# Key transposes of a pooled-attention kernel: one DMA transpose per head pair in place of one for two pairs

## The chip, the cores and the metric

The kernel runs on one core of one Trainium2 chip. The metric is the device time of one execution in microseconds (us). Five runs of the kernel before gave 418.2 to 424.3 us, with a median of 421.87 us. One execution was recorded by the hardware profiler, and every duration below comes from that execution or from its trace.

In the text PE is the matmul engine (TensorE), DVE the vector engine, ACT the scalar engine, POOL the GpSimd engine, and SP the sync engine, which here only issues DMAs. PEld is the weight load of PE.

## The reference, cut to what matters

Attention with queries pooled by two, over 8 batches, 8 heads, 1152 positions and head size 64, and then a feed-forward network with a product of two projections:

```python
q_pool = q.reshape(B, H, S // 2, 2, D).mean(axis=3)          # 576 pooled queries
scores = (1 / sqrt(D)) * q_pool @ k.transpose(0, 1, 3, 2)    # 576 x 1152 per head
attn = exp(scores - max) / sum
x = (attn @ v).transpose(0, 2, 1, 3).reshape(4608, 512)
out = ((x @ w1) * (x @ w2)) @ w3 @ w_out                     # 4608 x 512
```

Inputs and output are 32-bit floats. The kernel computes in 16-bit floats and sums in 32 bits.

## The kernel before, in words

**Tiling.** Two heads of one batch make a pair, so there are 32 pairs. For a pair, `scores` multiplies keys by pooled queries on PE (line 292). Both operands must have the head dimension on the partitions: `kT` holds the transposed keys of a pair (9 blocks of 128 columns; head 0 in partitions 0 to 63, head 1 in 64 to 127) and `qT` the transposed pooled queries. `expo` takes the exponential on ACT (line 302) of a chunk of 2 x 512 scores, `attend` multiplies the result by the values on PE (line 317), and `normalize` divides by the sum on DVE (lines 330, 334) and writes the result transposed into `xT` with DMA transposes from SP (lines 342, 345). The feed-forward network takes `xT` in units of 512 rows: `pa` and `pb` (line 411), their product `gT` (line 423), and the output rows `pp` (line 429), stored by SP (line 450).

**The order of the work.** It is written out by hand. The main loop has 108 iterations; each has three chunks of scores and exponentials, a listed number of `attend` matmuls, and up to two feed-forward groups. No engine reorders anything: each works through its own instructions in the order in which the loop emitted them, and waits at the first whose inputs are not ready. The framework derives the waits from the regions of tiles that an instruction reads and writes.

**How keys and queries get there.** Pairs 0 to 7 are transposed on PE. From pair 8 on two pairs P and P+1 are prepared together, by `prep_dma` (line 137), emitted about 1.95 pairs of scores ahead of pair P. In order, it does this:

1. `pool_q` (line 122), on POOL, adds neighbouring queries of both pairs into one tile `qp`.
2. Two copies on POOL (line 142), one for each pair, put the loaded keys `kst` into the block order of `kc`. Each waits for the landing of its own pair's keys.
3. SP issues one DMA transpose of `kc` into `kT` for both pairs (line 145, 18 blocks of 128 x 128) and then one of `qp` into `qT` (line 148, 9 blocks, since the two pairs' queries share partitions).

After it, `settled` (line 152) has POOL copy one element of `kT[P]` into a scratch cell. The value is not used; the copy makes POOL wait until the keys have landed transposed. Only then does POOL issue `load_two` for the next two pairs: two query loads, two value loads and two key loads (lines 82, 96, 89), which cast from 32 to 16 bits on the way. So POOL, SP and the DMA engines run a cycle, one turn for two pairs: loads, key copies, key transpose, the one-element copy, the next loads. `kc` has one buffer, `kT` and `qT` have two, `kst` and `vst` four.

Of the kernel before, what the change touches and what calls it, by code (L numbers as in the profile page):

```python
# [23 lines left out]
def kernel(  # L24
# [11 lines left out]
    nc = tc.nc  # L36
# [38 lines left out]
    kst, vst, qst, kT, qT, kTs, qTs, qps = {}, {}, {}, {}, {}, {}, {}, {}  # L75
# [38 lines left out]
    def pool_q(P, n=1):  # L114

        eng = nc.gpsimd if n == 2 else nc.vector
        pp, o = P // 2, 64 * (P % 2)
        if P % 2 == 0 or P == 1:
            qps[pp] = ab.tile([128, NJ, 2, D], FP16, tag="qp", bufs=2, name="qp")
        r = slice(o, o + 64 * n)  # L120
        src = qst[pp][r].rearrange("p u (c two) d -> p u c two d", two=2)
        eng.tensor_tensor(  # L122
            out=qps[pp][r].rearrange("p c u d -> p u c d"),
            in0=src[:, :, :, 0, :], in1=src[:, :, :, 1, :], op=ALU.add)

    def new_kq(P):
        if P % 2 == 0:
            kTs[P // 2] = ab.tile([128, 2, NJ, 128], FP16, tag="kT", bufs=2, name="kT")
            qTs[P // 2] = ab.tile([128, NJ, 128], FP16, tag="qT", bufs=2, name="qT")
        o = 64 * (P % 2)  # L130
        kT[P] = kTs[P // 2][:, P % 2]
        qT[P] = qTs[P // 2][:, :, o:o + 64]
# [4 lines left out]
    def prep_dma(P):  # L137

        pool_q(P, 2)
        for p in (P, P + 1):  # L140
            new_kq(p)
            nc.gpsimd.tensor_copy(  # L142
                out=new_kc(p).rearrange("p j u d -> p u j d").bitcast(mybir.dt.int32),
                in_=kst.pop(p).bitcast(mybir.dt.int32))
        nc.sync.dma_start_transpose(
            out=kTs[P // 2].rearrange("p t j f -> p (t j) f"),
            in_=kc2[P // 2].rearrange("p t j u d -> p (t j u d)"))
        nc.sync.dma_start_transpose(
            out=qTs[P // 2], in_=qps[P // 2].rearrange("p c u d -> p (c u d)"))

    def settled(P):
        nc.gpsimd.tensor_copy(out=seen, in_=kT[P][0:1, 0, 0:1])
# [1 line left out]
    kcs, kc2 = {}, {}  # L154

    def new_kc(P):
        if P % 2 == 0:
            kc2[P // 2] = ab.tile([128, 2, NJ, 2, D], FP16, tag="kc", bufs=1, name="kc")
        kcs[P] = kc2[P // 2][:, P % 2]
        return kcs[P]  # L160
# [241 lines left out]
    def ffn_groups(t):  # L402
# [70 lines left out]
        out=ident, in_=ident, compare_op=ALU.not_equal, fill=1.0,  # L473
# [102 lines left out]
    for it in range(NIT):  # L576
# [23 lines left out]
        if prepped < NPE:  # L600
            if it >= first_it(prepped) - (1 if prepped < 5 else 2):
                queue[0:0] = prep_groups(prepped)
                prepped += 1
                urgent = True
        elif prepped < NP and at >= prepped - 1.95:
            prep_dma(prepped)
            if loaded < NP:
                settled(prepped)
                load_two(loaded)
                loaded += 2  # L610
            prepped += 2
# [65 lines left out]
```

## Time and profile before

| what | before |
|---|---|
| median of 5 runs | 421.87 us (418.2 to 424.3) |
| profiled execution, its own time | 422.98 us |
| span of the profiled execution | 421.2 us |
| granted TensorE clock | 0.999 |
| PE busy | 409.2 us, 97% of the span |
| ACT busy | 326.9 us, 78% |
| DVE busy | 196.4 us, 47% |
| POOL busy | 121.0 us, 29% |
| moved by DMA | 59.76 MB |

The span is the stretch between the first and the last instruction that the profiler recorded; the execution's own time is 1.8 us more. "Busy" leaves out the time in which an engine only waits, branches or issues a DMA. The page also names a chain of work that ended last. It is found by going back from the last instruction to what released it, step by step, and where an engine waited even a little for a DMA, the chain goes off into what that DMA had waited for. So a large share of a line in the chain tells that work hangs on that line; it does not tell how long anyone waited for it. That stands in the view of waits, which adds up for every pair of waiter and releaser how long the waiter was idle.

### The profile page before, as it was taken

To read this page: it belongs to the slowest core of one execution; us is meant where nothing else is said; L and a number is where in the kernel's file an instruction comes from. 1 tells how busy PE (TensorE), PEld (TensorE's weight loads), DVE (VectorE), ACT (ScalarE), POOL (GpSimd) and SP (SyncE) were. 2 spreads that over 40 slices of the span, in tenths; PEclk is the share of its full clock that TensorE was granted. 3 is DMA by queue.
4 is the path that set the end of the run, shared out by engine and by line. 5 is a ranking of instruction groups with operands and counts; after the bars stand their busy time and mean duration, and the time that the engine had idled before them with its cause. 6 is when DMAs were issued, how large, how long until landed. Compare 5 with 4: busy or idle time off the path is not lost.

```text
span 421.2 us, 12709 instructions
## 1 busy us (share of the span) xinstructions
PE 409.2 (97%) x5507; PEld 272.3 (65%) x5507; DVE 196.4 (47%) x407; ACT 326.9 (78%) x357; POOL 121.0 (29%) x161
## 2 busy tenths in 40 slices
PE   8989999999999999999999999999999999999996
PEld 5567777766676577666765676666765866544443
DVE  2345656464545553555454534544455534613140
ACT  4899998988888888988888889897888889133332
POOL 6543431343434242331514242434333100000000
PEclk9999999999999999999999999999999999999999
DMA  8999999597989999897989998998989851050404
GB/s 188 202 207 193 200 205 202 99 150 129 171 147 190 142 154 173 128 161 134 130 129 206 136 178 159 175 137 152 182 145 155 133 125 23 14 115 2 100 2 100
DMA packets 95801, 59.76 MB, mean 142 GB/s; under 512 B 65152, under 2 KB 86144, under 8 KB 95744
## 3 DMA queue, kind: packets, MB, share of 16 engines
q0 software_dynamic: 26928, 32.97, 51.3%
q1 hardware_dynamic: 68656, 25.84, 35.1%
q8 instruction: 43, 0.70, 0.7%
q10 hardware_dynamic: 160, 0.13, 0.1%
q14 instruction: 14, 0.11, 0.1%
HBM read 67.11 MB, written 9.44 MB: 182 GB/s over the span
## 4 chain that ended last, share of the span: by engine, by line
DMA 60%; PE 24%; POOL 8%; ACT 3%; issue 2%; SPq 1%; DVE 1%; POOLq 0%; ACTq 0%
DMA kst<-in_k_dram 32%; DMA kT<-kc 15%; DMA qst<-in_q_dram 7%; PE pa L411 5%; PE pp L429 5%; PE pb L411 5%; DMA vst<-in_v_dram 4%; PE psc L292 3%; PE po L317 3%; ACT er L302 3%; POOL qst L82 2%; POOL kc L142 2%; POOL vst L96 2%; DMA er<-in_k_dram 1%; DMA qT<-qp 1%
## 5 line engine op out<-in xcount | busy, mean ns | idle before, releaser
L302 ACT ACTIVATE er<-psc 128x1024 f16<-128x1024 f32 x324 | 307.5, 1028 | 43.9 <-PE psc L292 43.6
L317 PEld LDWEIGHTS <-er 128*128 128x128 f16 x2880 | 103.3, 97 | 21.9 <-issue 5.8
L317 PE MATMUL po<-vt,er 128*128 128x65 f16 x2880 | 110.3, 193 | 0.0
L292 PE MATMUL psc<-qT,kT 64*128 64x512 f16 (+7 forms) x1152 | 96.7, 288 | 4.6 <-ACT er L302 2.2
L423 DVE TENSOR_TENSOR gT<-pb,asb 128x512 f16<-128x512 f32 x72 | 49.8, 692 | 56.4 <-PE pb L411 55.7
L411 PE MATMUL pa<-xT,w1sb 128*128 128x512 f16 x288 | 74.2, 380 | 0.0
L411 PE MATMUL pb<-xT,w2sb 128*128 128x512 f16 x288 | 74.1, 380 | 0.0
L429 PE MATMUL pp<-T,gT 128*128 128x256 f16 (+1 forms) x488 | 67.9, 292 | 0.0
L292 PEld LDWEIGHTS <-kT 64*128 64x128 f16 x1152 | 45.6, 94 | 29.2 <-issue 10.2
L429 PEld LDWEIGHTS <-gT 128*128 128x128 f16 x488 | 45.7, 98 | 18.5 <-issue 3.7
L421 DVE COPY asb<-pa 128x512 f32<-128x512 f32 x56 | 38.7, 692 | 39.9 <-PE pa L411 38.8
L411 PEld LDWEIGHTS <-w2sb 128*128 128x128 f16 x288 | 26.4, 98 | 32.7 <-issue 3.9
L411 PEld LDWEIGHTS <-w1sb 128*128 128x128 f16 x288 | 25.1, 98 | 30.1 <-issue 6.2
L122 POOL TENSOR_TENSOR qp<-qst 128x1152 f16<-128x1152 f16 x12 | 28.2, 2354 | 46.8 <-DMA qst<-in_q_dram 33.8
L441 DVE TENSOR_SCALAR osb<-pp 128x256 f32<-128x256 f32 x49 | 20.8, 425 | 39.3 <-PE pp L429 33.2
L330 DVE RECIPROCAL rz<-po 128x5 f32<-128x5 f32 x64 | 12.4, 194 | 50.2 <-PE po L317 49.8
L142 POOL COPY kc<-kst 128x576 int32<-128x576 int32 x24 | 16.1, 671 | 58.0 <-DMA kst<-in_k_dram 58.0
L334 DVE TENSOR_TENSOR xn<-po,rz 128x320 f16<-128x320 f32 x64 | 31.5, 492 | 2.5 <-DVE rz L330 0.3
L96 POOL DMA_DIRECT2D vst<-in_v_dram x32 | 23.4, 742 | 11.2 <-DMA w3h<-in_moe_w_dram 3.0
L438 ACT ACTIVATE osb<-pp 128x512 f32<-128x512 f32 (+1 forms) x12 | 7.0, 579 | 24.0 <-PE pp L429 20.6
L89 POOL DMA_DIRECT2D kst<-in_k_dram x31 | 22.8, 751 | 9.2 <-DMA kst<-in_k_dram 2.6
L419 ACT COPY asb<-pa 128x512 f32<-128x512 f32 x16 | 9.4, 585 | 16.5 <-PE pa L411 16.5
(42 smaller groups left out, 151.5 us busy)
## 6 DMA issues: line engine op xcount, KB each, us to landing
vst<-in_v_dram POOLq DMA_DIRECT2D x32, 288.0 KB, 10.2
out_dram<-osb SPq DMA_DIRECT2D x70, 128.0 KB, 2.5
kst<-in_k_dram POOLq DMA_DIRECT2D x31, 288.0 KB, 12.3
qst<-in_q_dram POOLq DMA_DIRECT2D x31, 288.0 KB, 6.6
w3h<-in_moe_w_dram POOLq DMA_DIRECT2D x3, 512.0 KB, 15.0
xT<-in_moe_w_out_dram POOLq DMA_DIRECT2D x4, 256.0 KB, 10.2
w1sb<-in_moe_w_dram POOLq DMA_DIRECT2D x2, 512.0 KB, 15.7
w2sb<-in_moe_w_dram POOLq DMA_DIRECT2D x2, 512.0 KB, 16.9
```

Source lines behind the costliest of these rows:

```text
L89: nc.gpsimd.dma_start(out=kst[P].rearrange("p u j d -> p u (j d)"), in_=k[b, h0:h0 + 2].rearrange("u (p j) d -> p u (j d)", j=NJ))
L96: nc.gpsimd.dma_start(out=vst[P].rearrange("p u j d -> p u (j d)"), in_=v[b, h0:h0 + 2].rearrange("u (p j) d -> p u (j d)", j=NJ))
L122: eng.tensor_tensor(out=qps[pp][r].rearrange("p c u d -> p u c d"), in0=src[:, :, :, 0, :], in1=src[:, :, :, 1, :], op=ALU.add)
L142: nc.gpsimd.tensor_copy(out=new_kc(p).rearrange("p j u d -> p u j d").bitcast(mybir.dt.int32), in_=kst.pop(p).bitcast(mybir.dt.int32))
L292: nc.tensor.matmul(t[:, u, o:o + ln].rearrange("p (c f) -> p c f", f=64), kT[P][s, j, :], qT[P][s, f0 // 64:(f0 + ln) // 64], start=True, ...
L302: nc.scalar.activation(out=er[:, :, r:r + CH], in_=psc.pop(c), func=AF.Exp, bias=0.0, scale=SCALE)
L317: nc.tensor.matmul(po[P, u][:, VW * x:VW * x + D + 1], er[:, u, r:r + 128], vts[P % 4][:, u, j, 0:D + 1], start=(m == 0), stop=(m == 44), ...
L334: nc.vector.tensor_tensor(out=xn[:, P % 2, :, u, :], in0=acc[:, :, 0:D], in1=rz.to_broadcast([128, 5, D]), op=ALU.mult)
L411: nc.tensor.matmul(p, w[:, mc, ft * 128:ft * 128 + 128], xT[:, mc, t0:t0 + 512], start=(mc == 0), stop=(mc == NC - 1))
L421: nc.vector.tensor_copy(out=asb[ft], in_=p)
L423: nc.vector.tensor_mul(out=gT[:, ft, :], in0=p, in1=asb.pop(ft))
L429: nc.tensor.matmul(p[:, 0:n], gT[:, ft, 128 * i:128 * i + 128], T16[:, ft, n * s:n * s + n], start=(ft == 0), stop=(ft == NF - 1))
```

## The change

In `prep_dma` the one DMA transpose of the keys of two pairs becomes two, one for each pair, and the transpose of the queries, which came after the keys, now stands between them. `settled(P)`, which is not edited, reads the first element of `kT[P]`, which the first of the two writes. Loads, copies, tiles, buffers and the place of `prep_dma` in the loop stay as they are.

```diff
@@ prep_dma @@
             nc.gpsimd.tensor_copy(
                 out=new_kc(p).rearrange("p j u d -> p u j d").bitcast(mybir.dt.int32),
                 in_=kst.pop(p).bitcast(mybir.dt.int32))
-        nc.sync.dma_start_transpose(
-            out=kTs[P // 2].rearrange("p t j f -> p (t j) f"),
-            in_=kc2[P // 2].rearrange("p t j u d -> p (t j u d)"))
-        nc.sync.dma_start_transpose(
-            out=qTs[P // 2], in_=qps[P // 2].rearrange("p c u d -> p (c u d)"))
+        for p in (P, P + 1):
+            nc.sync.dma_start_transpose(
+                out=kT[p], in_=kcs[p].rearrange("p j u d -> p (j u d)"))
+            if p == P:
+                nc.sync.dma_start_transpose(
+                    out=qTs[P // 2], in_=qps[P // 2].rearrange("p c u d -> p (c u d)"))
```

## The prediction

> **What bounds the kernel now.** I first read the busy times, then the waits, then the chain. The table of stretches, cut at 80 us (the first DMA transposes) and at 357 us (the last scores), gives for each engine its busy time:
>
> ```profile
> core 0: us, PE busy (x) PEld busy (x) DVE busy (x) ACT busy (x) POOL busy (x), PEclk, DMA share, GB/s
> 80.00:357.00 277.00, 275.06 (x3963) 186.79 (x3961) 135.87 (x278) 239.34 (x253) 89.58 (x113) 1.00 0.95 147
> ```
>
> In the 277 us in which the changed lines run, PE is idle for 277.00 − 275.06 = 1.94 us, at a clock of 1.00. The waits of PE alone, in the same stretch, have one line only:
>
> ```profile
> PE psc L292 <- DMA qT<-qp: 1.9, 4, 1.0
> ```
>
> Scores waited four times for the transposed queries. So PE, with 99.3% of the stretch, sets the pace. The change takes no work from PE, so at most these 1.94 us can be had. But the waits of all engines, and those of SP's queue, show that a second thing runs nearly as slowly:
>
> ```profile
> POOL seen L152 <- DMA kT<-kc: 62.7, 11, 6.6
> POOL kc L142 <- DMA kst<-in_k_dram: 58.0, 22, 5.8
> ...
> SPq L145 <- POOL kc L142: 121.8, 12, 12.8
> ```
>
> POOL waits 62.7 us for key transposes and 58.0 us for keys: no work of its own, but the cycle of loads and transposes going round. The chain, in order of time, shows one turn of it (start, duration, what):
>
> ```profile
> 283.78 0.68 POOL kc L142
> ...
> 284.47 4.67 DMA kT<-kc
> ...
> 289.26 0.18 POOL seen L152
> ...
> 289.72 1.25 POOL qst L82 x2
> 290.98 1.44 POOL vst L96 x2
> 292.42 0.68 POOL kst L89
> 293.09 11.85 DMA kst<-in_k_dram
> ```
>
> The keys of the second pair are copied, both pairs are transposed (4.67 us), POOL sees it and issues six loads, the last of which lands 15.2 us after the first was issued. From the issue of the key transpose for pair 16 (169.57 us) to that for pair 30 (330.14 us) seven turns take 160.57 us, 22.94 each. PE begins the scores of pair 16 at 180.24 and those of pair 30 at 337.74; less the 1.92 us of waits this is (157.50 − 1.92) / 7 = 22.23 per turn. So the cycle is 0.7 us a turn slower than PE. It used up its lead: the queries of pairs 8 to 16 landed 2.5 to 5.8 us before their scores, those of pairs 18, 22, 26 and 30 at the moment of use, with PE idle for 0.16, 0.31, 1.05 and 0.40 us. The page's 97% of PE and this cycle are both near the bound, and **the sign of the change hangs on whether the cycle gets shorter or longer**.
>
> **The change part by part.** Issue time on SP first:
>
> ```profile
> L145 SPq DMA_TRANSPOSE kT<-kc x12: 2652/2712/3817, 81.5 to 330.1; - x12
> ...
> DMA to landing us min/median/max: 4.7/5.2/6.5
> ...
> L148 SPq DMA_TRANSPOSE qT<-qp x12: 1350/1370/1629, 84.2 to 332.9; - x12
> ...
> DMA to landing us min/median/max: 3.3/4.5/4.8
> ```
>
> 18 blocks take 2.71 us to issue and 9 blocks 1.37, so two transposes of 9 cost 2 x 1.37 = 2.74: 0.03 us more, nothing. A transpose of 9 key blocks isn't in the trace; the query transpose has the same number and size of blocks and lands after 3.3 to 4.8, so I take that row. *Above*, the price is that of a transpose beside loads (below).
>
> *The first key transpose* needs only the first copy. For pair 26 that copy ended at 283.43 and the second at 284.45, so it is issued 1.0 us earlier. Over the last eight turns the first copy ended 1.0 to 3.3 us ahead of the second, 1.4 as a rule. *The query transpose* comes behind 1.37 us of issue and not behind 2.71. For pair 26: 283.45 + 1.37 + 0.04 = 284.86, landed after its own 3.41 at 288.27, where it was 290.64. The same sum with each turn's own durations gives for pairs 18, 22, 26 and 30 a landing 2.8, 3.3, 2.4 and 2.6 us earlier. Each is more than PE waited there (0.16 to 1.05). So all four waits go, even if nothing adds up from turn to turn. The next release of these scores is then PE itself: **1.9 us off**.
>
> *The wait of the one-element copy* is now for the first key transpose. With pair 18: issued at 192.95 (first copy's end 192.93), landed 3.4 later at 196.35 where the joint one landed at 199.02. The loads start 2.7 us earlier; with the slow 4.8 it is 1.3 us. In front of that copy POOL still waits for the second pair's keys (193.61) and copies them until 194.33, so that side doesn't bind. Queued behind it are the six loads alone, and these want to start.
>
> *The second key transpose* is issued last, after the queries and the second copy: for pair 18 at 195.7, and it would land at about 199.1 undisturbed. Its reader, the scores of pair 19, begins at 213.68. Today the joint transpose lands 12.1 to 17.5 us before the second pair's scores, which covers any duration in the trace. *The `xT` transposes and the stores* behind it on SP are not delayed: the three transposes together are issued by 197.1, where the two were issued by 198.50. This queue stood with its head at line 145 for 121.8 us in 12 waits, and the `xT` transposes were issued up to 11.9 us after their data was ready; an earlier head is their gain.
>
> *What is added* is traffic beside traffic. The loads' first packets follow their issue by about 1.5 us, so part of the second key transpose is in flight with them. Its price from both sides: nothing, if it is through by then; else by the `xT` transposes. One issued clear of the loads at 288.70 landed after 2.5 us; the three issued with the loads at 177.3 to 180.2 took 10.7 to 12.8. The loads pay too: the six took 17.25 us from first issue to last landing with those three beside them (176.36 to 193.61), and 13.5 in the quickest turn (88.62 to 102.12), whose first two `xT` transposes had been issued before. So at most (17.25 − 13.5) / 2 = 1.9 us for one transpose of this size; I take 1.0, the middle, as about half of it overlaps. A turn thus changes by −2.7 + 1.0 = −1.7 us (between −2.7 and −1.3 + 1.9 = +0.6), to 21.2 us, under PE's 22.23. The lead grows instead of shrinking, and PE is the only bound.
>
> The Trainium skill, "DMA: Bandwidth & Descriptors", section "Rules for kernel authors", speaks against splitting: many small transfers should be merged into a large one; its section on the anatomy of a DMA puts a constant 2.0 us on each. By that rule a turn would get about 2 us longer, an estimate from that page, and the kernel some 14 us slower (7 turns of 2.0). The rows of issue and landing above say that a constant exists but overlaps: transposes of 9 and of 18 blocks land 3.3 and 4.7 us after issue at best, and one is issued while the one before is in flight.
>
> **The sum.** The profiled execution: 422.98 − 1.92 = 421.06 us (span 419.3). It is 1.1 us above the median of the five runs; the same 1.9 off the median of 421.87 gives **420.0 us**. Its own range is 418.6 to 421.5. It is less than 1%, which is about what a measurement of this kernel can tell from no change.
>
> **Rivals.**
> *The cycle gets longer (13%).* The first key transpose is in flight while the second pair's keys still land, and the second with the loads. It decides from the point where the first takes more than 4.67 + 1.4 = 6.1 us to land, or where the loads stretch by more than the 2.7 us that they start earlier. For it: `xT` transposes beside loads take up to 12.8 us, and the cycle has no lead from pair 18 on, so each us per turn is paid: +0.9 over seven turns is 7 x 0.9 = 6.3 us on top of today's waits, **428 us**. Against it: the second keys landed 0.3 to 2.6 us after the first copy, and the first packets of a transpose came about 1.0 us after issue, so they hardly meet.
>
> *The change doesn't do what it says (4%).* If waits went by whole tiles, the one-element copy and pair P's scores would wait for the second transpose, which now comes behind the queries: 1.37 us later per turn, 7 x 1.37 = 9.6 us, **431.5 us**. Against it: the `pa` matmul of a unit began at 255.38, before the last transpose into the same `xT` tile, of other columns, landed at 255.72.
>
> *Nothing is had (10%).* The waits on the queries go, but another comes in their place, such as the `xT` transposes, which now share the engines longer: the one that unit 4 needs landed at 254.34, and its user started at 256.03. Then **421.9 us**.
>
> *More is had (5%).* Unprofiled executions may lose more to this wait than 1.9 us; the five differ by 6.1 us. Removing three times as much would give **416.2 us**. Against it: the profiled run is itself the second slowest.
>
> **How the numbers follow.** The forecast has the remaining 68%. Faster by over 1% (under 417.7) is the last rival and a tail of the forecast: 0.07. Slower by over 1% (over 426.1) is the first two: 0.17. Within 1%: 0.76. The range runs from 417.5, a little under the forecast's own end, to 427.0, inside the longer cycle: it leaves out the upper half of that one, the whole-tile case and most of the largest gain, some 15%.
>
> **What would show it.** Right: PE's wait for the queries gone from the list; POOL's wait at line 152 cut from 5.7 us to about 3 a time; turns of the cycle at 21 to 22 us; PE idle under 0.5 us between 80 and 357. Wrong: scores that wait for `kT` or `qT` for over 2 us in total, loads that take over 18 us a turn, or first key transposes that land after more than 6 us.

## The result, and the profile after

The changed kernel takes 419.19 us in the median of 43 runs (417.95 to 422.41); the kernel before takes 421.80 us in the median of 80 (417.71 to 426.15). The medians are 2.6 us apart, a quotient of 0.9938. The ratio is 0.9954, with a 95% interval of 0.9939 to 0.9968; like every ratio below it leaves out, as slow, the runs that took over 1.5% more than the quickest of their kernel, here 13 of the 80 of before and none of the changed kernel. So the change is worth 0.5 to 0.6%. The forecast was 420.0 / 421.87 = 0.9956. The spread has shrunk too: 8.4 us between the extremes before, 4.5 us after.

The same stretch of the changed kernel, busy time by engine:

```profile
core 0: us, PE busy (x) PEld busy (x) DVE busy (x) ACT busy (x) POOL busy (x), PEclk, DMA share, GB/s
80.00:357.00 277.00, 276.98 (x3988) 187.81 (x3985) 138.22 (x279) 239.83 (x252) 89.08 (x112) 1.00 0.94 148
```

PE is idle for 0.02 us where it was idle for 1.94. The view of PE's waits over the whole span (waiter, releaser, us in total, times, longest) begins with

```profile
PE psc L293 <- ACT er L303: 2.6, 9, 0.5
PE spin L194 <- DVE hot L70: 1.1, 1, 1.1
PE spin L194 <- DVE w3T L389: 0.5, 1, 0.5
PE t L170 <- ACT er L303: 0.3, 1, 0.3
```

and holds no DMA at all. The page's chain of work that ended last, by engine, says the same in another way:

```profile
PE 88%; ACT 5%; DMA 3%; issue 1%; DVE 1%; POOL 1%; SPq 0%; ACTq 0%
```

Before it was

```profile
DMA 60%; PE 24%; POOL 8%; ACT 3%; issue 2%; SPq 1%; DVE 1%; POOLq 0%; ACTq 0%
```

The four small waits had led the chain off into the loads. 60% of a chain was worth 0.5% of the time.

The waits of POOL and SP's queue for the cycle of loads and transposes, and the row of the key transposes:

```profile
POOL kc L142 <- issue: 46.4, 11, 5.4
POOL seen L153 <- DMA kT<-kc: 41.6, 11, 10.5
...
POOL kc L142 <- DMA kst<-in_k_dram: 10.9, 11, 2.1
```

```profile
SPq L146 <- POOL kc L142: 50.6, 7, 20.3
...
SPq L146 <- PE psc L293: 21.4, 4, 7.5
```

```profile
L146 SPq DMA_TRANSPOSE kT<-kc x24: 1272/1328/2205, 80.6 to 312.9; - x24
...
DMA to landing us min/median/max: 3.3/3.7/5.8
```

POOL's wait for the keys is as long as before (46.4 + 10.9 us, part of it now put down to "issue"); the wait of the one-element copy has gone from 62.7 to 41.6. SP waits for the key copies 50.6 us, where it waited 121.8.

Against the profiled execution of before, the span is 4.6 us shorter, and only part of that is the change. The scores of pair 8 begin at 89.25 us where they began at 91.84, 2.6 us earlier, before the first changed instruction matters. In two more profiles of the kernel before they begin at 89.45 and 90.14, so this start varies by itself. From the scores of pair 8 to those of pair 30 it takes 243.35 us where it took 245.90: 2.55 us, the change's own. That is more than the idle time of 1.92 us: each of the four waits makes its turn of scores 0.16 to 0.18 us longer than the gap itself. Behind pair 30 the new execution is 0.55 us longer.

**The lead**, from the landing of queries and first keys to the first scores of the pair (worked out from landings and matmuls in the traces):

| pair | 8 | 12 | 16 | 18 | 22 | 26 | 30 |
|---|---|---|---|---|---|---|---|
| before, us | 3.0 | 5.8 | 3.4 | 0.0 | 0.0 | 0.0 | 0.0 |
| after, us | 3.0 | 9.1 | 12.1 | 12.9 | 17.8 | 13.0 | 17.8 |

It stops growing at 17.8 us: in the later turns the key transposes also stand in SP's queue until PE's scores are through (the 21.4 us above) or behind stores that wait for their data.

### The profile page after: what moved, and what is told of

The parts are those of the page before. It is cut to its first block, busy times and chain, and to the rows that moved or that the text cites. A ratio compares the mean times of both kernels' runs of the same rounds, so it can differ in the third digit from the quotient of the medians.

```text
span 416.6 us, 12735 instructions
## 1 busy us (share of the span) xinstructions
PE 406.5 (98%) x5507; PEld 271.7 (65%) x5507; DVE 196.9 (47%) x407; ACT 326.7 (78%) x357; POOL 120.8 (29%) x161
## 3 DMA queue, kind: packets, MB, share of 16 engines
q0 software_dynamic: 26928, 32.97, 50.6%
## 4 chain that ended last, share of the span: by engine, by line
PE 88%; ACT 5%; DMA 3%; issue 1%; DVE 1%; POOL 1%; SPq 0%; ACTq 0%
PE po L318 20%; PE psc L293 19%; PE pa L412 16%; PE pb L412 15%; PE pp L430 15%; ACT er L303 5%; PE pT L396 3%; DMA qst<-in_q_dram 2%; DMA out_dram<-osb 1%; DMA er<-in_k_dram 1%; PE t L170 0%; PE w3t L384 0%; POOL vst L96 0%; DVE qp L122 0%; POOL kst L89 0%
## 5 line engine op out<-in xcount | busy, mean ns | idle before, releaser
L293 PE MATMUL psc<-qT,kT 64*128 64x512 f16 (+7 forms) x1152 | 94.8, 285 | 3.0 <-ACT er L303 2.6
L442 DVE TENSOR_SCALAR osb<-pp 128x256 f32<-128x256 f32 x49 | 20.8, 425 | 38.1 <-PE pp L430 31.8
L142 POOL COPY kc<-kst 128x576 int32<-128x576 int32 x24 | 15.9, 664 | 57.3 <-issue 46.4
L439 ACT ACTIVATE osb<-pp 128x512 f32<-128x512 f32 (+1 forms) x12 | 7.0, 579 | 24.0 <-PE pp L430 20.4
L89 POOL DMA_DIRECT2D kst<-in_k_dram x31 | 22.6, 744 | 9.3 <-DMA w1sb<-in_moe_w_dram 3.2
## 6 DMA issues: line engine op xcount, KB each, us to landing
kst<-in_k_dram POOLq DMA_DIRECT2D x31, 288.0 KB, 12.1
```

The costliest lines, as they stand in the source:

```text
L89: nc.gpsimd.dma_start(out=kst[P].rearrange("p u j d -> p u (j d)"), in_=k[b, h0:h0 + 2].rearrange("u (p j) d -> p u (j d)", j=NJ))
L293: nc.tensor.matmul(t[:, u, o:o + ln].rearrange("p (c f) -> p c f", f=64), kT[P][s, j, :], qT[P][s, f0 // 64:(f0 + ln) // 64], start=True, ...
L442: nc.vector.tensor_scalar_mul(out=osb, in0=p[:, 0:n], scalar1=1.0 / (SCL * SCL))
```

## The experiments

The experiments ask what made the lead grow. Two theories were tested. **Release:** the lead grows because the loads are issued earlier in each turn, as the prediction had it. **Order:** it is enough that queries and keys land earlier within a turn, whenever the loads start. All ratios are to the kernel before, run beside on the same chip. The table takes each turn of a profile apart: (a) from the last landing of the loads to the issue of the first key transpose, negative when that is issued before the last keys land; (b) from there to the issue of the first load; (c) from there to the last landing. The rows are means over the 11 turns of a profile, less those (none to two) in which the next key transpose was issued over 3 us after the last landing because SP's queue stood at something else; shorter holds of this kind are still in them. Over all 11 turns the changed kernel has 20.86 us.

| kernel | a | b | c | turn, us | ratio (95%) |
|---|---|---|---|---|---|
| before | 0.74 | 6.14 | 15.72 | 22.60 | 1 |
| before_again | 0.74 | 5.92 | 15.76 | 22.42 | |
| before_third | 0.76 | 6.08 | 15.74 | 22.57 | |
| after | -0.23 | 4.46 | 16.12 | 20.35 | 0.9954 (0.9939 to 0.9968) |
| after_again | -0.65 | 4.28 | 16.66 | 20.29 | 0.9931 (0.9903 to 0.9959) |
| joint_q_first | 0.96 | 5.89 | 14.24 | 21.09 | 0.9906 (0.9872 to 0.9939) |
| q_first_again | 0.85 | 6.10 | 14.16 | 21.11 | 0.9918 (0.9888 to 0.9947) |
| split_wait_second | -0.83 | 7.31 | 14.65 | 21.13 | 0.9929 (0.9900 to 0.9958) |
| split_q_last | -0.21 | 4.33 | 16.31 | 20.44 | 0.9957 (0.9927 to 0.9987) |
| split_later_2us | -1.10 | 6.05 | 15.21 | 20.17 | 0.9920 (0.9892 to 0.9948) |
| split_both_copied | 1.47 | 4.16 | 16.79 | 22.41 | 1.0110 (1.0060 to 1.0160) |
| joint_later_1us | 0.76 | 6.52 | 15.05 | 22.33 | 1.0033 (0.9987 to 1.0078) |
| joint_later_4us | 0.74 | 10.15 | 13.59 | 24.48 | 1.0414 (1.0342 to 1.0486) |

Three profiles of the kernel before give 22.4 to 22.6 us, so differences of 1 us in a turn mean something. Over the first five turns alone (pair 8 to pair 18), where no turn is left out, the order is the same: 22.1 to 22.6 us in the three of before and 22.5 in `split_both_copied`, 20.8 to 20.9 in `joint_q_first`, `q_first_again` and `split_wait_second`, 20.2 in `split_later_2us`, and 19.8 to 20.0 in the changed kernel (twice) and `split_q_last`.

### One part alone: the order, and the loads' wait

`joint_q_first`: one key transpose as before, the query transpose ahead of it.

```diff
+        nc.sync.dma_start_transpose(
+            out=qTs[P // 2], in_=qps[P // 2].rearrange("p c u d -> p (c u d)"))
         nc.sync.dma_start_transpose(
             out=kTs[P // 2].rearrange("p t j f -> p (t j) f"),
             in_=kc2[P // 2].rearrange("p t j u d -> p (t j u d)"))
-        nc.sync.dma_start_transpose(
-            out=qTs[P // 2], in_=qps[P // 2].rearrange("p c u d -> p (c u d)"))
```

> One key transpose for two pairs as before, but the query transpose is issued ahead of it. The cycle of loads is not shortened: the loads still wait for both pairs' keys. If the shorter cycle makes the gain, the turns stay at 22 to 23 us, the lead of pairs 18 to 30 stays under 3 us, and PE's waits in scores only shrink (the joint keys landed 1.1 to 2.9 us before the queries in those turns): ratio 0.996 to 0.999, with a wider spread of runs than the changed kernel's. If the order within a turn alone makes it, the ratio is that of the changed kernel, 0.995, with no wait of PE and the same narrow spread.

Neither theory had the shorter turn. The ratio is 0.9906, and the profile's turns are 21.1 us: shorter by 1.5, though the loads still wait for both pairs' keys. The whole difference is in the loads (14.24 where it was 15.72). The query transpose depends on the loaded queries alone, which land some 8 us ahead of the last keys, so here it is issued 1.4 us and more ahead of the key transpose, in 10 of 12 turns while keys still land. SP then reaches the `xT` transposes 1.4 us sooner behind the keys, and less is left beside the loads. From pair 20 on the lead is 10 to 14 us.

`split_wait_second`: the changed kernel, with the loads held for the second key transpose.

```diff
-                settled(prepped)
+                settled(prepped + 1)
```

> The changed kernel, but the one-element copy reads the second pair's keys, so the loads wait for both key transposes. If the shorter cycle makes the gain, turns go back to 22.5 to 23 us and the lead of pairs 18 to 30 falls from 12 to 18 us to 2 to 5 us; PE's waits are under 0.5 us, since the queries still land 2.4 to 3.3 us earlier in the turn: ratio 0.995 to 0.998. If the release of the loads alone counts, waits of about 2 us are back: ratio 1.000.

The turns did not go back: 21.1 us, a lead of 6.5 to 12.7 us from pair 18 on, ratio 0.9929. The loads start later than in the changed kernel (a + b is 6.5, where that has 4.2), and finish sooner once started (14.65, where that has 16.12). Waiting for the first keys alone is not what the gain needs.

`split_q_last`: two key transposes, then the queries.

```diff
         for p in (P, P + 1):
             nc.sync.dma_start_transpose(
                 out=kT[p], in_=kcs[p].rearrange("p j u d -> p (j u d)"))
-            if p == P:
-                nc.sync.dma_start_transpose(
-                    out=qTs[P // 2], in_=qps[P // 2].rearrange("p c u d -> p (c u d)"))
+        nc.sync.dma_start_transpose(
+            out=qTs[P // 2], in_=qps[P // 2].rearrange("p c u d -> p (c u d)"))
```

> Two key transposes, then the queries, as late in the turn as before; the loads wait for the first key transpose alone. If the shorter cycle makes the gain: turns of 20 to 21 us, a lead over 8 us from pair 18 on, no wait of PE for queries, ratio 0.995. If the place of the queries in the order makes it: waits of about 2 us as before, ratio 1.000.

0.9957 and 20.4 us: as the first theory said. The place of the queries isn't needed either. It has a small price in the first turn, where there is no lead yet; the only wait of PE for a DMA in that profile is for the queries of pair 8:

```profile
PE psc L292 <- DMA qT<-qp: 1.0, 1, 1.0
```

### The second keys' landing

What the three kernels and the changed one share is that 9 blocks of transposes are under way before the second pair's keys are copied. `split_both_copied` takes that away from the changed kernel: the second pair's keys, which land last, are copied first. It changes one more thing. Both copies now stand behind the last landing, so (a) is 1.47 us, 0.7 more than in the kernel before.

```diff
         for p in (P, P + 1):
             new_kq(p)
+            new_kc(p)
+        for p in (P + 1, P):
             nc.gpsimd.tensor_copy(
-                out=new_kc(p).rearrange("p j u d -> p u j d").bitcast(mybir.dt.int32),
+                out=kcs[p].rearrange("p j u d -> p u j d").bitcast(mybir.dt.int32),
                 in_=kst.pop(p).bitcast(mybir.dt.int32))
```

> The changed kernel with the second pair's keys copied before the first pair's, so that no transpose can start before both pairs' keys have landed; the loads still wait for the first key transpose alone. In the profiles so far the changed kernel's turn is made up of -0.2 us from the keys' last landing to the first key transpose, 4.5 us from there to the first load, and 16.1 us of loads; the kernel before has 0.7, 6.1 and 15.7. If the early start in the gap between the copies makes the shorter turn: back to 22 us and more, a lead under 4 us from pair 18 on, ratio 0.996 to 1.000. If the early release of the loads makes it: 0.8 + 4.5 + 16.1 = 21.4 us, a lead that still grows, ratio 0.993 to 0.996.

The turns are 22.4 us, as before the change, although the loads are issued 1.25 us earlier than there (a + b is 5.63 against 6.88). 1.07 of it comes back as longer loads. As a test between the two readings this is weaker than expected: with the measured 1.47 for (a) in place of 0.8, the sum for the early release is 22.1 us, close to the measured 22.4. The ratio misses both expected ranges. The kernel is slower than before, by 1.1%, with a new wait in PE's list:

```profile
PE pa L414 <- DMA xT<-xn: 4.7, 2, 2.9
```

The units of the feed-forward network that begin at 213.78 and 259.07 us waited for `xT` transposes. Every group of these from 151 to 317 us was in flight beside the loads. Here is the row over the stretch from 80 to 340 us:

```profile
L345 SPq DMA_TRANSPOSE xT<-xn x24: 1212/1462/2982, 86.5 to 335.1; - x24
...
DMA to landing us min/median/max: 2.5/10.9/13.8
```

The changed kernel's `xT` transposes take as long (up to 12.1 us from 143 us on), but with its lead they are issued earlier in PE's time and no wait comes of it. So the early release without the early start gained next to nothing in the turn, and the kernel lost time. How the two share the shorter turn is told by `joint_q_first` and `split_wait_second`: their loads are issued 6.85 and 6.48 us after the last landing (a + b), hardly earlier than the 6.88 of before, and their turns are 1.5 us shorter; with the early release on top, in the changed kernel, it is 2.25.

### How much a delay costs

Idle copies on POOL ahead of the loads; two of them in the kernel before (`joint_later_1us`), eight (`joint_later_4us`), and four in the changed kernel (`split_later_2us`). A copy took 0.54 us.

```diff
+    pad = const.tile([128, 2, 432], mybir.dt.int32)
...
                 settled(prepped)
+                for _ in range(2):
+                    nc.gpsimd.tensor_copy(out=pad[:, 1], in_=pad[:, 0])
```

> The kernel before with two idle copies on POOL ahead of the loads, 0.5 us each, so that each turn is 1.0 us longer. If the cycle of loads had become the bound, as the prediction says, PE now waits in most turns from pair 12 on: 7 to 11 us on top of the waits of before, ratio 1.015 to 1.025. If the cycle has slack that the waits hide, or goes by something else than POOL's release, the ratio stays under 1.005.

> The kernel before with eight idle copies on POOL ahead of the loads, 4.3 us a turn. If a delay of the loads is fully paid: turns of 26 us, PE waits of 30 us and more, ratio 1.07. If part of it comes back because the transposes on SP are through before the loads start: the shortest stretch of loads seen so far is 12.3 us, 3.4 below the mean of before, so turns of at least 23.2 us, waits of 5 to 25 us, ratio 1.01 to 1.05.

> The changed kernel with four such copies ahead of the loads, 2.0 us a turn. The free turns of the changed kernel were 20.2 us, so they get 22.2 us, PE's own pace: the lead of pairs 18 to 30 falls from 12 to 18 us to 1 to 5 us, PE waits under 1 us, ratio 0.995 to 0.998. If the true margin is smaller, waits of 2 us and more are back and the ratio is 1.000 or above.

`joint_later_1us`: the waits in most turns didn't come. The ratio is 1.0033, with an interval that holds 1, and the turn no longer than that of before (22.33). The loads were issued 0.7 us later after the transposed keys' landing (part of the copies lies beside POOL's own 0.3 us ahead of the first load) and took 0.67 less. But this profile is of the quickest of the twelve runs (419.46 us). Four of them, which the ratio leaves out, took 426.3 to 428.3 us, longer than any of the 34 of the kernel before beside them (up to 425.3). So the delay may well cost something in some executions; none of these was profiled. `joint_later_4us` shows where that ends: with the loads 4.0 us later (b), they took 2.1 us less, and the turn grew by 1.9. PE waited for queries five times between 80 and 357 us:

```profile
PE psc L294 <- DMA qT<-qp: 16.1, 5, 3.8
```

In `split_later_2us`, the changed kernel with its loads 1.9 us later after the first keys' landing, the turn stays at 20.2 us, the lead over 10 us from pair 18 on, and PE idles 0.02 us; turns of 22.2 us and a lead of 1 to 5 had been expected. The margin is larger than the first theory gave it: the loads took 15.21 us where they took 16.12.

### Without the hold

`joint_no_hold`: the kernel before without the one-element copy, so that the loads are issued right behind the key copies.

```diff
             if loaded < NP:
-                settled(prepped)
                 load_two(loaded)
```

> The kernel before without the one-element copy: POOL issues the loads as soon as it has copied the keys, so key and query transposes run beside the loads. If loads and transposes only share the engines and the lead grows: key transposes take 8 to 13 us, turns are 19 to 21 us, PE doesn't wait, ratio 0.995. If transposes beside loads lengthen the cycle, as the rival of the longer cycle has it: turns over 23 us and waits of several us for kT, ratio 1.01 or more.

The ratio is 1.0229 (1.0165 to 1.0292); the six runs took 429.56 to 439.12 us. In the profiled one, of 438.39 us, the key transposes ran beside the loads altogether:

```profile
L145 SPq DMA_TRANSPOSE kT<-kc x12: 2690/8628/11054, 81.3 to 330.2; - x12
...
DMA to landing us min/median/max: 4.7/16.6/22.4
```

```profile
PE psc L292 <- DMA qT<-qp: 17.8, 4, 15.3
```

A transpose that takes 5.2 us in the median took 16.6, and six loads 15.8 to 22.9 us. (In these loads some time is POOL's own: it waited 23.2 us in total for the copies of values before it could load more.) Yet the turns, from one key transpose's issue to the next, are 22.6 us, as before, where over 23 had been expected, and pairs 8 to 30 take 247.97 us, which lies among the three profiles of before (245.90 to 249.22). The loss is the one wait of 15.3 us ahead of pair 8: the first key transpose took 22.4 us, and there is no lead yet. So this run doesn't show the longer cycle of the first rival. What this execution lacked was the hold in the first turn; in the changed kernel, which keeps it for the first half, that half landed 4.2 us after its issue. Whether the quicker runs lose their time at the same place isn't known.

### The two good orders side by side, and the spread of before

> The changed kernel once more, on the chip of the runs below. PE has no idle time left in the stretch from 80 to 357 us, so nothing but the start varies: median 418.5 to 419.5 us, ratio 0.993 to 0.996, lead of pairs 18 to 30 again over 9 us.

> The joint transpose behind the queries, beside the changed kernel on one chip. If PE is the only bound of both, they agree within 0.2% though their turns differ in make. If a shorter stretch of loads is worth something beyond PE's waits, this one is faster by 0.3% or more.

On one chip the changed kernel has 418.66 us and the joint transpose behind the queries 418.54 us in the median, with overlapping intervals: no difference. PE idles 0.02 us in the one and 0.38 in the other. Nothing beats the changed kernel, and in this stretch nothing of this kind can.

> The kernel before, another profile. If its spread of 418 to 426 us comes from the waits for queries, its PE idle time between 80 and 357 us goes with its time: about 419 us with none, and 1 us of idle for each us above that.

> The kernel before, a third profile, for the same relation: its time less its PE idle time between 80 and 357 us is 418 to 420.5 us in all profiles of it.

PE's waits for queries in these two profiles of the kernel before:

```profile
PE psc L292 <- DMA qT<-qp: 2.3, 4, 1.5
```

```profile
PE psc L292 <- DMA qT<-qp: 3.7, 3, 3.1
```

Their own times are 421.74 and 423.92 us, with 2.36 and 3.76 us of PE idle time from 80 to 357 us. Less the idle time the three profiles of before give 421.04, 419.38 and 420.16. The expected 418 to 420.5 misses the first, which had begun pair 8 by 1.7 and 2.4 us later than the others. The changed kernel, 418.39 less 0.02, gives 418.4.

The time from the scores of pair 8 to those of pair 30 leaves the start out, and there the sum closes. It is 243.34 to 243.39 us in all six profiled executions in which PE didn't wait between them (`after`, `after_again`, `joint_q_first`, `split_wait_second`, `split_q_last`, `split_later_2us`), whatever their turns, and 245.90, 246.33 and 249.22 us in the three of the kernel before. The 2.55 and 2.98 us on top in the first two are idle time of 1.92 and 2.33 us and 0.17 us for each of four waits. The 5.87 us of the third are 3.73 us of idle time, 0.5 for three waits, and 1.7 for the clock, which was granted at 0.50 for the 3.4 us from 291.18 us on, right behind a wait of 3.1 us. So PE is the only bound there, and the waits, which vary from execution to execution, make the difference. The start is another part of the spread, and wasn't followed.

## Why the prediction was right, and where its reasons were not

**What bounds the kernel:** right. PE's idle time in the stretch was the gain to be had, and it went from 1.94 to 0.02 us. The ratio of the forecast, 0.9956, lies in the interval. That the size fits so closely is partly luck: 1.94 us is one execution's idle time, and two more profiles of the kernel before have 2.36 and 3.76. By the medians of all runs the gain is 2.6 us, so the rival with more to be had had a ground, though not three times as much. "At most these 1.94 us" was also a little low: from pair 8 to pair 30 the change got 2.55 us, since each wait cost 0.17 us more than its idle time; PE's own pace from pair 16 to pair 30 is 22.13 us a turn in the changed kernel, where 22.23 was worked out.

**The four waits go within their own turn:** they went, and PE's list has no DMA left. Splitting costs nothing in issue time (1.33 us a half, where 1.37 was taken), and the first half lands 3.3 to 5.1 us after issue, half of them within 3.4 (3.4 was taken; two are above the bound of 4.8). That the waits go "even if nothing adds up from turn to turn" isn't shown by any run: by pair 18 the lead had grown to 12.9 us, and `split_q_last`, with the queries as late in the turn as before, has no wait there either.

**The constant cost by the skill's rule:** the Trainium skill's "DMA: Bandwidth & Descriptors" ("Rules for kernel authors") would have had the transposes merged; of the 2 us a turn that were worked out from its constant nothing is to be seen, and the turn got 2.25 us shorter. The constant stands in the page's section on DMAs issued from GpSimd, and these are issued by SP. From the issue of the first to the landing of the last, the three transposes of a turn in `split_both_copied` took 6.9 us in the mean, and so did the two of the kernel before with the same 27 blocks: in one queue a transpose more cost no constant.

**The turn, -2.7 + 1.0 = -1.7 us:** the sizes held. Release after the last landing (a + b) went from 6.88 to 4.23, that is -2.65; the loads grew by 0.40 (by 0.94 in the second profile); together -2.25 (-1.74 over all eleven turns). But the step that gives the whole gain of a turn to the earlier release, the wait of the one-element copy, failed in part. With the release as before (`joint_q_first`) or 0.4 us earlier (`split_wait_second`) the turn was still 1.5 us shorter, so about 0.8 of the 2.25 us is left for the release. Where the release came earlier without the early start (`split_both_copied`), the turn fell by 0.2, with a copy of 0.7 us more in it. What goes with most of the gain is that 9 blocks of transposes start before the last keys are copied. Why that helps, that less is then left to share the DMA engines with the loads, is read from the shorter loads (14.24 and 14.65 us, where they took 15.72) and wasn't tested by itself.

**"Each us per turn is paid":** right for a turn that really gets longer. In `joint_later_4us`, with turns of 24.48 us, pairs 8 to 30 took 25.5 us more than without waits, 2.3 a turn, about what the turn exceeds PE's pace of 22.12 us by. What failed is to count a later or earlier issue of the loads as so much more or less of a turn: of 0.7 us nothing reached the turn of the profiled execution, and of 4.0 us 1.9 did. The rival's 428 us itself, a turn 0.9 us longer, wasn't met by any run.

**Rivals:** waits by whole tiles didn't happen: the one-element copy started 0.1 us after the first key transpose landed, with the second still in flight in all 11 turns. The `xT` transposes, named as a wait that could take the place of the old one, did so in `split_both_copied`, not in the changed kernel, whose lead covers them; the prediction didn't count on that. Against the longer cycle it has the first packets of a transpose about 1.0 us after its issue; in that trace it is 1.2 us for each of the twelve.

**What would show it:** PE idle under 0.5 us, yes (0.02). POOL's wait at the one-element copy about 3 us a time: 3.8, and 3.1 without one of 10.5 us, in which SP's queue held the key transposes behind output stores. Turns of 21 to 22 us: 20.9 over all eleven, 20.35 in the table, a little under.

## What to carry to other kernels

When the engine that sets the pace is nearly always busy, its idle time is about the ceiling of any change to the feeding of it, whatever share of the chain the feeders have (here each wait cost 0.17 us more than its gap, and one of 3 us lowered the clock as well); and a feeder that is 2% too slow costs little until its lead is used up, then shows as a few short waits and as spread between runs. To shorten such a feeding cycle, start its next stage in the time in which the last transfer is still landing, by splitting it or by putting first what is ready first. Issuing the following loads earlier was worth less here, since they then took longer beside the transposes, and letting them share altogether cost a wait of 15 us in the first turn, which has no lead, in the execution that was profiled.

## What the runs showed of the hardware that was not expected

**Transposes beside loads take several times as long, and so do stores.** 18 blocks landed 4.7 us after issue at best when no loads were in flight, and after a median of 16.6 us beside six casting loads (`joint_no_hold`). It isn't the transposes' own: in the profile of before, between 80 and 340 us, the stores of output rows landed after a median of 2.4 us clear of the loads (9 stores) and of 6.8 us with over half of their flight beside them (27).

**A long wait of PE lowers its clock for a while.** In `joint_no_hold` PE waited 15.3 us in one piece ahead of pair 8. The stretches of that profile:

```profile
80.00:120.00 40.00, 24.71 (x356) 15.30 (x354) 12.33 (x25) 20.59 (x22) 15.32 (x19) 0.83 1.11 129
120.00:160.00 40.00, 39.13 (x518) 25.88 (x515) 19.63 (x40) 33.20 (x36) 15.37 (x18) 1.00 1.25 145
```

The granted clock is 0.83 in the first and 1.00 in the next. In the trace's record of the clock it is 0.50 from 94.59 to 108.25 us, that is from 5.1 us into the wait to 3.5 us behind its end. Shorter waits show it too: 0.50 for 3.4 us behind the wait of 3.1 us in `before_third`, and for 3.4 to 6.8 us about the end of four of the five waits of 2.9 to 3.8 us in `joint_later_4us`. Behind the fifth, and behind the waits of 2.9 and 1.8 us in `split_both_copied`, the clock stayed at 1.00.

**Joint key transposes take 4.7 us or about 6.** In the profile of before six of twelve took 5.8 to 6.5 us, the other six 4.7. In the trace's DMA packets each of the six slow ones, and none of the fast ones, has a packet of the instruction queue beginning between 1 us after its issue and its landing, of 16 KB and 0.9 to 1.5 us. At 150.22 us, for example, one of 0.93 us is followed by twenty transpose packets of 256 bytes that take 1.4 us each, where 0.02 is usual. In the two more profiles of the kernel before it is the same: all nine that took 5.7 us or more have such a packet, and none of the others. That the instruction load holds up the transpose is read from this coincidence; no run tested it.
